# Gating the first branch: from the last stage's first passes into the third stage's second half

## The chip, the cores and the metric

The kernel runs on 1 core of a Trainium2 chip. The metric is the device time in microseconds (us) of one execution. Five engines work side by side, each in its own order: PE (TensorE: matmuls), DVE (VectorE), ACT (ScalarE), POOL (GpSimd) and SP (SyncE, which here only issues DMA transfers). An engine takes its instructions strictly in turn: if the next one waits for a semaphore, everything behind it on that engine waits too.

## The reference

```
x: 2048 x 1024;  h = layernorm(x) over the last axis
g = sigmoid(sum(x * gate_w))                        # one gate per row
a = Cs_re @ (x @ Ch_re.T) - Cs_im @ (x @ Ch_im.T)   # first branch: Fourier mixing
u = gelu(h.T @ w1 + b1)                             # w1: 2048 x 3584
b = (u @ w2 + b2).T                                 # second branch; w2: 3584 x 2048
out = g * a + (1 - g) * b
```

Everything is float32.

## The kernel before, in words

**Four stages.** The first two compute the first branch `a` and store it to the output tensor `out_dram` (they use the symmetry of the Fourier matrices; a check of it, `verdict`, picks a general path for other matrices, which isn't run with these inputs). The third (`Up`, tiles named `u_...`) computes `u` and stores it to DRAM; the last (`Down`, tiles `o_...`) multiplies `u` by `w2` and adds the result, scaled by `hgate` = 1 - g, onto `out_dram`. Before a block of `out_dram` can be added to, it must have been multiplied by the gate.

**Passes.** Third and last stage are block products, 4 x 4 blocks of the weight (`W`) by 4 x 2 of the other operand (`R`), done with a bilinear scheme of 26 products where the plain way takes 32. Each product is a pass j = 0 to 25; its operands are sums and differences of blocks, made by DVE from tiles that SP (some by POOL) loads, or by accumulating DMA. A float32 operand is split into a high part (ACT, `L653`) and a low part (DVE, `L658` and `L660`), and each product of tiles is three matmuls (`L1056` to `L1058`). A pass has 4 blocks of k by 7 row tiles in the third stage, and 7 by 4 in the last (three passes there, 3, 15 and 22, are split once more). When a pass ends, ACT (`plain_copy`, L1101) or DVE (`fused`, L1109) reads its PSUM banks into `u_c` or `o_c` tiles before PE may use these banks again. There are 8 banks; a third-stage pass uses 7, a last-stage pass 4. In the third stage ACT then applies gelu (L1363), and POOL stores `u_c` to `u`.

**The gate.** In pass 7 to 13 of the third stage the gates are computed (`row_gate`, `gates`: tiles `gate`, `hgate`, `ngate`, `bgate`; ACT part at L1522). `gated(i, h, key)` then treats one half row block of the first branch: SP loads 128 x 512 floats of `out_dram` into a tile `g` (through `load`, L626), ACT multiplies by the gate and adds `bgate` (L1505), and POOL stores the tile back (through `store`, L636). 16 row blocks by 2 halves make 32 such pieces.

**What sets the order.** The program is first written down as a list of tasks. Each carries a key, the step it belongs to; a step is one block of k, so a third-stage pass is 4 steps and a last-stage pass 7. `during(j, key)` is called at the start of pass j and adds what runs beside it; `GATED_AT` and `GATED_STEP` say from which pass on the pieces come and how many steps lie between them. A planner (`Graph.schedule`) then plays the whole program through with costs of its own and writes down each engine's instructions in the order in which they started there. A task is due in relation to the place of its key on PE's line. A load is taken to land when its bytes have passed at `DMA_RATE` (400000 bytes a us) and 3.5 us more (`DMA_LATENCY`) have gone by; what reads the tile is placed behind that. Tiles share slots (`f`: 39 of 1024 floats a partition, `h`: 24 of 512, `ps`: 8 banks); a load needs a free slot.

Of the kernel before, what the change touches and what calls it, by code (L numbers as in the profile page):

```python
# [20 lines left out]
NS = S // P  # L21
# [10 lines left out]
DMA_RATE = 400000.0  # L32
SPARE = 2
DMA_LATENCY = 3.5
ADD_LATENCY = 1.5
LOAD = 14.0
WAIT = 0.5
# [8 lines left out]
def act(n):  # L46
    return 0.10 + n * 0.86e-3
# [188 lines left out]
STATS_AT, STATS_STEP = ("y", 1), 4.5  # L236
GATE_AT, GATE_STEP = 7, 1.5
VERDICT_AT = 21
GATED_AT, GATED_STEP = 0, 2
H_LEAD, H_EACH = 25, 1.3  # L240
O_ORDER = [24, 6, 17, 15, 0, 13, 12, 2, 25, 1, 16, 10, 5, 14, 4, 23, 3, 7, 11, 21, 18, 22, 9, 8, 19, 20]
O_SUMS = signs([
# [42 lines left out]
class Buf:  # L285
# [3 lines left out]
    def __init__(self, kind, name, t=None, parts=1, dtype=F32):  # L289
        self.kind, self.name, self.t, self.parts, self.dtype = kind, name, t, parts, dtype  # L290
        self.writer = [None] * parts
        self.readers = [[] for _ in range(parts)]
        self.taker = self.reading = self.next = None
        self.users = set()
# [53 lines left out]
class Task:  # L348
    def __init__(self, seq, key, engines, fn, nbytes):
        self.seq, self.key, self.engines, self.fn, self.nbytes = seq, key, engines, fn, nbytes  # L350
        self.deps, self.after, self.need, self.behind, self.bufs = set(), [], [], [], {}
        self.order = (key, seq)
        self.engine = self.bank = None

    def __lt__(self, o):
        return self.order < o.order


class Graph:
# [72 lines left out]
    def schedule(self):  # L432
# [7 lines left out]
        at, dma, now = 0, 0.0, 0.0  # L440
# [36 lines left out]
        def start(t, e):  # L477
            nonlocal dma
            t.engine, t.start = e, now
            if t.bank:  # L480
                t.bank.reading = t
            order.append(t)
            for b in t.need:
                b.index = free[b.slot].pop(0)
                waiting[b.kind].remove(t)
            idle[e] = now + t.engines[e]
            end = idle[e]
            if t.nbytes:
                dma = max(dma, now) + t.nbytes / DMA_RATE
                end = dma + DMA_LATENCY + (ADD_LATENCY if t.engines[e] == 0.9 else 0)  # L490
            heapq.heappush(events, idle[e])
            t.end = end
            heapq.heappush(events, end + HOP)
            heapq.heappush(done, (end + HOP, t.seq, t))
            for s in t.after:
                unborn[s] -= 1
                if not unborn[s]:
                    s.ready = max(d.end for d in s.deps) + HOP
                    for o in s.engines:
                        if o in soon and len(s.engines) == 1:  # L500
                            soon[o].append(s)
# [10 lines left out]
        while events:  # L512
# [3 lines left out]
            while done and done[0][0] <= now:  # L516
                t = heapq.heappop(done)[2]
# [8 lines left out]
            if idle["PE"] <= now and at < len(pe) and not left[pe[at]] and has_slots(pe[at]):  # L526
                start(pe[at], "PE")
                at += 1
            for e, heap in ready.items():
                held = []  # L530
                while heap and idle[e] <= now and len(held) < 60:
                    t = heapq.heappop(heap)
# [17 lines left out]
def arm(  # L550
# [19 lines left out]
    g = Graph(SLOTS)  # L570
# [43 lines left out]
    def slot(n, name, dtype=F32):  # L614
        return View(Buf("f" if n > H else "h", name, None, 1, dtype), 0, n)
# [7 lines left out]
    def load(key, v, src, r=(), queue="SP"):  # L623
        q = {"SP": nc.sync, "ACT": nc.scalar}[queue]
        dst = (lambda: v.ap.rearrange("p (c j) -> p c j", j=H)) if len(src.shape) == 3 else lambda: v.ap
        g.add({queue: 0.06}, key, lambda e: q.dma_start(dst(), src), r=r, w=(v.reg,), nbytes=P * v.n * 4)  # L626
# [100 lines left out]
    class Bilinear:  # L727
# [57 lines left out]
        def during(self, j, key):  # L785

            if (self.name, j) == STATS_AT:
                stats(key, STATS_STEP)
# [521 lines left out]
    class Up(Bilinear):  # L1310
# [20 lines left out]
        def during(self, j, key):  # L1331
            if fast and j == VERDICT_AT:
                verdict()
            if j == GATE_AT:
                load_consts(key)
                for row in range(NS):
                    row_gate(row, key + GATE_STEP * row, View(self.h[row], 0, D))
                gates(key + GATE_STEP * NS)
# [29 lines left out]
    class Down(Bilinear):  # L1368
# [11 lines left out]
        def source(self, x_, b, k):  # L1380
# [2 lines left out]
                return w2[i * P:(i + 1) * P, c:c + H], ()  # L1383
            i, h = (b // 2) * 7 + k, b % 2
            return u_dram[i].t[:, h * H:(h + 1) * H], [(u_dram[i], h)]

        def during(self, j, key):
            if j == GATED_AT:
                for n in range(2 * NS):
                    gated(n // 2, n % 2, key + GATED_STEP * n)  # L1390

        def back(self, b, j):
            return j == len(self.out) - 1 or next(i for i in self.ends[b] if i >= j) == len(self.out) - 1
# [66 lines left out]
    def load_consts(key):  # L1460
        src = bass.AP(tensor=gate_w.tensor, offset=gate_w.offset, ap=[[0, P], [1, D]])
        prod = View(Buf("h", "xgw", None, 1, mybir.dt.bfloat16), 0, D)
        load(key, GW, src)
        g.add({"ACT": act(D) + 0.25}, key, lambda e: nc.scalar.activation(prod.ap, GW.ap, AF.Copy, accum_out=sgw.t),
              r=(GW.reg,), w=(prod.reg, sgw))

    def stats(key, each):
        load(key, View(b12_sb, 0, NF + NS), b12)
        for row in range(NS):
            row_stats(row, key + each * row)  # L1470
        rstds(key + each * NS)
# [22 lines left out]
    def row_gate(k, key, v):  # L1494

        prod, col = View(Buf("h", f"xg{k}", None, 1, mybir.dt.bfloat16), 0, D), slice(k, k + 1)
        g.add({"DVE": dve(D)}, key, lambda e: nc.vector.scalar_tensor_tensor(
            prod.ap, v.ap, 1.0, GW.ap, op0=ALU.mult, op1=ALU.mult, accum_out=zg.t[:, col]),
            r=(v.reg, GW.reg), w=(prod.reg, zg))

    def gated(i, h, key):

        v, reg, cols = slot(H, f"g{i}_{h}"), (out_dram[i], h), slice(h * H, (h + 1) * H)
        load(key, v, out_dram[i].t[:, cols], (reg,))
        g.add({"ACT": act(H) + 0.08}, key, lambda e: nc.scalar.activation(  # L1505
            v.ap, v.ap, AF.Identity, bias=bgate.t[:, i:i + 1], scale=gate.t[:, i:i + 1]), r=(v.reg, gate, bgate), w=(v.reg,))
        store(key + 0.5, out_dram[i].t[:, cols], reg, v)
# [760 lines left out]
    def verdict():  # L2268
        n = len(kept)
        parts, sums16 = const(n, "parts"), Buf(None, "sums16", consts.tile([P, n], BF16, tag="sums16", name="sums16"))  # L2270
        total, test, usual = const(n, "total"), const(3, "test"), [const(1, f"usual{i}") for i in range(2)]
        at = {what: i for i, what in enumerate(kept)}

        def fill(_):
            for b, few in zip(usual, (SPECIAL, FEW)):
                nc.vector.memset(b.t, 1.0)
                nc.vector.memset(b.t[:few, :], 0.0)

        g.add({"DVE": 0.3}, -1, fill, w=usual)
        for what, i in at.items():  # L2280
            m = counted[what]
            assert m == len(kept[what].writer), (what, m)
            g.add({"ACT": 0.5}, step, lambda e, i=i, what=what: nc.scalar.activation(
                kept[what].t, kept[what].t, AF.Copy, accum_out=parts.t[:, i:i + 1]), r=(kept[what],), w=(kept[what], parts,))

        def masked(e):
            for b, what in zip(usual, ("odd", "even")):
                i = at[what]
                nc.vector.tensor_mul(parts.t[:, i:i + 1], parts.t[:, i:i + 1], b.t)

        g.add({"DVE": 0.2}, step, masked, r=(*usual, parts), w=(parts,))
        g.add({"DVE": 0.1}, step, lambda e: nc.vector.tensor_copy(sums16.t, parts.t), r=(parts,), w=(sums16,))
        ps = Buf("ps", "ps_verdict")
        g.add({"PE": 0.1}, step, lambda e: nc.tensor.matmul(ps.t[:, :n], ones[:, :P], sums16.t, start=True, stop=True), r=(sums16,), w=(ps,))

        def decide(e):
            v, t, a, b = nc.vector, total.t, test.t[:, :1], test.t[:, 1:2]

            def col(what):
                return t[:, at[what]:at[what] + 1]  # L2300

            v.tensor_scalar(t, ps.t[:, :n], 1.0, None, op0=ALU.mult)
            v.scalar_tensor_tensor(a, col("rest"), LEAST, col("seq_main"), op0=ALU.mult, op1=ALU.is_lt)
            v.scalar_tensor_tensor(b, col("hid_rest"), LEAST, col("hid_main"), op0=ALU.mult, op1=ALU.is_lt)
            v.tensor_mul(a, a, b)
            for what, most in (("seq_main", 1e30), ("hid_main", 1e30), ("odd", 0.5), ("even", 0.5), ("all", 0.5)):
                v.tensor_scalar(b, col(what), most, None, op0=ALU.is_lt)
                v.tensor_mul(a, a, b)
            v.tensor_scalar(b, a, -1.0, 1.0, op0=ALU.mult, op1=ALU.add)
            v.tensor_copy(bad, b)  # L2310

        g.add({"DVE": 1.0}, step, decide, r=(ps,), w=(total, test, Buf(None, "bad", bad)))
# [6 lines left out]
    for t in g.schedule():  # L2319
        for b in t.need:  # L2320
            pool, n = pools[b.slot]
# [98 lines left out]
```

## Time and profile before

| what | value |
|---|---|
| median of 3 runs | 1250.75 us (1249.62 to 1253.84) |
| profiled execution, its own time | 1252.64 us |
| its span, first to last instruction | 1250.6 us |
| mean granted TensorE clock | 0.992 |
| instructions | 17645 |
| DMA traffic | 347.35 MB, mean 278 GB/s |

The profile is of one execution. A group row names line, engine, operation, written and read tiles (buffer numbers left out), shapes and count. In the timeline a row starts with its start and its duration in us; brackets give how long the engine had been idle before it and what ended that. "PEclk" is the clock that the throttle granted, as a share of full speed; the DMA share is the mean busy share of the 16 DMA engines (it can pass 1 a little, since a packet's time is counted where it started).

### The profile page before, as it was taken

How to read it: one execution, taken by the hardware profiler on the slowest of the kernel's cores; microseconds unless marked ns; L12 is line 12 of the kernel's file. 1: busy time of each engine (PE TensorE's matmuls, PEld its weight loads, DVE VectorE, ACT ScalarE, POOL GpSimd, SP SyncE). 2: the span in 40 equal slices, each digit the busy share in tenths (PEclk: the TensorE clock that was granted, in tenths of full speed). 3: DMA queues.
4: the chain of work that ended last, by engine and by line, in shares of the span. 5: the costliest groups of instructions: out<-in, count | busy, mean ns of one | idle time of the engine just before them, and what ended most of it. 6: DMA issues, size and time to landing. Idle time of an engine off the chain costs nothing.

```text
span 1250.6 us, 17645 instructions
## 1 busy us (share of the span) xinstructions
PE 1221.7 (98%) x5640; PEld 983.3 (79%) x5647; DVE 1152.9 (92%) x1998; ACT 699.2 (56%) x1252; POOL 211.1 (17%) x325
## 2 busy tenths in 40 slices
PE   8999999899999999999999999999999999999997
PEld 5678756688888888887787887887788889888886
DVE  8999978999998899989999689898999989999995
ACT  7852697584743424534635567756545546665632
POOL 0000010312130220211202233213120111231212
PEclk9999999999999999999999999999899999999999
DMA  9999772989577798989967999999993687899655
GB/s 376 402 360 408 279 203 72 300 308 358 198 272 267 261 343 310 342 306 354 358 248 242 403 406 361 299 320 321 273 292 121 178 217 210 231 247 289 131 139 104
DMA packets 142282, 347.35 MB, mean 278 GB/s; under 512 B 17378, under 2 KB 20322, under 8 KB 142179
## 3 DMA queue, kind: packets, MB, share of 16 engines
q1 hardware_dynamic: 109762, 256.39, 57.8%
q0 software_dynamic: 32272, 89.67, 26.1%
q8 instruction: 46, 0.75, 0.2%
q14 instruction: 58, 0.47, 0.1%
q10 hardware_dynamic: 144, 0.07, 0.0%
HBM read 264.40 MB, written 81.66 MB: 277 GB/s over the span
## 4 chain that ended last, share of the span: by engine, by line


## 5 line engine op out<-in xcount | busy, mean ns | idle before, releaser
L1056 PE MATMUL ps_u_p<-u_p_r_hi,u_p_w_hi 128*128 128x512 f32 x728 | 284.7, 391 | 2.0 <-DVE u_c L1109 2.0
L1058 PE MATMUL ps_u_p<-u_p_r_hi,u_p_w_lo 128*128 128x512 f32 x728 | 283.3, 389 | 0.0
L1057 PE MATMUL ps_u_p<-u_p_r_lo,u_p_w_hi 128*128 128x512 f32 x728 | 283.3, 389 | 0.0
L1056 PE MATMUL ps_o_p<-o_p_r,o_p_w 128*128 128x512 f32 x654 | 257.3, 393 | 7.3 <-DVE o_c L1109 4.3
L1057 PE MATMUL ps_o_p<-o_p_r,o_p_w 128*128 128x512 f32 x654 | 256.0, 391 | 0.0
L1058 PE MATMUL ps_o_p<-o_p_r,o_p_w 128*128 128x512 f32 x654 | 255.9, 391 | 0.0
L653 ACT ACTIVATE u_p_w_hi<-u_W_p 128x896 fp32r<-128x896 f32 x104 | 97.4, 949 | 125.0 <-DVE u_W_p L618 36.9
L1056 PEld LDWEIGHTS ps_u_p<-u_p_r_hi,u_p_w_hi 128*128 128x128 f32 x728 | 136.6, 188 | 34.1 <-DVE u_c L1109 6.2
L1058 PEld LDWEIGHTS ps_u_p<-u_p_r_hi,u_p_w_lo 128*128 128x128 f32 x728 | 136.6, 188 | 28.8
L1057 PEld LDWEIGHTS ps_u_p<-u_p_r_lo,u_p_w_hi 128*128 128x128 f32 x728 | 136.7, 188 | 28.0
L1056 PEld LDWEIGHTS ps_o_p<-o_p_r,o_p_w 128*128 128x128 f32 x654 | 123.7, 189 | 36.4 <-DVE o_c L1109 6.6
L1058 PEld LDWEIGHTS ps_o_p<-o_p_r,o_p_w 128*128 128x128 f32 x654 | 123.7, 189 | 26.0
L1057 PEld LDWEIGHTS ps_o_p<-o_p_r,o_p_w 128*128 128x128 f32 x654 | 123.9, 189 | 25.2
L653 ACT ACTIVATE o_p_w<-o_W_p 128x512 fp32r<-128x512 f32 x164 | 100.9, 625 | 62.1 <-DVE o_W_p L621 21.0
L653 ACT ACTIVATE o_p_r<-o_R_p 128x512 fp32r<-128x512 f32 x157 | 95.7, 623 | 67.7 <-DVE o_R_p L621 37.6
L636 POOL DMA_DIRECT2D u<-u_c x126 | 68.6, 545 | 288.9 <-DVE u_c L1109 133.0
L660 DVE TENSOR_TENSOR o_p_r<-o_R_p,o_p_r 128x512 fp32r<-128x512 f32 x157 | 107.0, 686 | 8.6 <-ACT o_p_r L653 8.5
L1611 PE MATMUL ps_fq<-fc,fx_f 128*128 128x256 f32 (+1 forms) x368 | 101.6, 422 | 4.6 <-DVE fx_h L618 3.4
L1109 DVE SCALAR_TENSOR_TENSOR u_c<-ps_u_p,u_c 128x512 f32<-128x512 f32 x161 | 105.3, 684 | 0.4
L1611 PEld LDWEIGHTS ps_fq<-fc,fx_f 128*128 128x128 f32 x368 | 70.7, 193 | 28.8 <-issue 13.4
L618 DVE TENSOR_TENSOR u_W_p<-u_W_p,u_W_p 128x896 f32<-128x896 f32 x72 | 77.2, 1085 | 5.8 <-DMA u_W_p<-in_w_dram 5.8
L631 POOL DMA_DIRECT2D o_W_p<-in_w_dram x50 | 46.3, 941 | 210.6 <-DVE o_p_w L658 57.1
(289 smaller groups left out, 1980.8 us busy)
## 6 DMA issues: line engine op xcount, KB each, us to landing
u_W_p<-in_w_dram SPq DMA_DIRECT2D x124, 448.0 KB, 6.7
o_W_p<-in_w_dram SPq DMA_DIRECT2D x160, 256.0 KB, 6.6
o_R_p<-u SPq DMA_DIRECT2D x140, 256.0 KB, 6.2
fc<-in_ct_dram SPq DMA_DIRECT2D x64, 512.0 KB, 9.2
u<-u_c POOLq DMA_DIRECT2D x126, 256.0 KB, 6.3
u_c<-u SPq DMA_DIRECT2D x70, 256.0 KB, 6.7
o_W_p<-in_w_dram POOLq DMA_DIRECT2D x50, 256.0 KB, 7.1
out_dram<-o_c POOLq DMA_DIRECT2D x44, 256.0 KB, 8.1
```

Of the source, the lines that this page charges most:

```text
L618: g.add({"DVE": dve(o.n)}, key, lambda e: nc.vector.tensor_add(o.ap, a.ap, b.ap), r=(a.reg, b.reg), w=(o.reg,))
L631: g.add({"POOL": 0.9}, key, lambda e: nc.gpsimd.dma_start(dst(), src, accum_op=ALU.add), r=(v.reg, *r), w=(v.reg,), nbytes=2.2 * P * v.n * 4)
L636: g.add({queue: 0.6 if queue == "POOL" else 0.06}, key, lambda e: q.dma_start(dst, v.ap), r=(v.reg,), w=(reg,) if reg else (), nbytes=P * ...
L653: g.add({"ACT": act(v.n)}, key, lambda e: nc.scalar.activation(hi.ap, v.ap, AF.Copy, scale=-1.0 if negate else 1.0), r=(v.reg,), w=(hi.reg,))
L660: nc.vector.tensor_sub(lo.ap, v.ap, hi.ap.bitcast(F32))
L1056: nc.tensor.matmul(bank.ap, wh.ap[:, c], rh.ap[:, e], start=a, stop=False, skip_group_check=True)
L1057: nc.tensor.matmul(bank.ap, wh.ap[:, c], rl.ap[:, e], start=False, stop=False, skip_group_check=True)
L1058: nc.tensor.matmul(bank.ap, wl.ap[:, c], rh.ap[:, e], start=False, stop=b, skip_group_check=True)
L1109: lambda e: nc.vector.scalar_tensor_tensor(o.ap, ps.ap, scale, o.ap, op0=ALU.mult, op1=ALU.add),
L1611: nc.tensor.matmul(b.ap[:, c0:c0 + r.shape[-1]] if r.shape[-1] < H else b.ap, w, r, start=begin, stop=end, skip_group_check=True)
```

## The change

The 32 calls of `gated` are made in the third stage from pass 13 on, 1.5 steps apart (48 steps, so up to pass 24 of 25), and no longer in the last stage from pass 0 on, 2 steps apart. Their loads get a margin: the planner takes them to land 5 us later than other loads. Nothing else is edited; the planner then orders all engines anew.

```
+MARGIN = 5.0
...
-GATED_AT, GATED_STEP = 0, 2
+GATED_AT, GATED_STEP = 13, 1.5
...
 class Task:
+        self.margin = 0.0
...
 Graph.schedule, start():
-                end = dma + DMA_LATENCY + (ADD_LATENCY if t.engines[e] == 0.9 else 0)
+                end = dma + DMA_LATENCY + t.margin + (ADD_LATENCY if t.engines[e] == 0.9 else 0)
...
 class Up:
         def during(self, j, key):
             if fast and j == VERDICT_AT:
                 verdict()
+            if j == GATED_AT:
+                for n in range(2 * NS):
+                    gated(n // 2, n % 2, key + GATED_STEP * n)
...
 class Down:
-        def during(self, j, key):
-            if j == GATED_AT:
-                for n in range(2 * NS):
-                    gated(n // 2, n % 2, key + GATED_STEP * n)
...
 def gated(i, h, key):
         load(key, v, out_dram[i].t[:, cols], (reg,))
+        g.tasks[-1].margin = MARGIN
```

Three places in the order show it. In the names, `u_p13_w_0_hi` is the high part of W, block 0, of pass 13 of the third stage, `g1_0` the gate's piece of row block 1, half 0; the numbers at the end count tiles. Code lines behind the edit are one or two higher in the changed kernel.

ACT in the last stage, from the end of pass 5's copies to the operands of pass 7, before:

```order
L1452 ACTIVATE o_c2_2_7969<-o_c2_2_7969,hgate_81 128x512
L653 ACTIVATE o_p7_w_0_8011<-o_W0_p4_0_6931 128x512
L1505 ACTIVATE g14_0_7936<-g14_0_7936,bgate_80,gate_79 128x512
L653 ACTIVATE o_p7_r_0_8024<-o_R4_p4_0_7005 128x512
L653 ACTIVATE o_p7_r_1_8031<-o_R4_p4_1_7048 128x512
L653 ACTIVATE o_p7_w_1_8039<-o_W0_p7_1_7797 128x512
```

and now:

```order
L655 ACTIVATE o_p7_w_0_7982<-o_W0_p4_0_6977 128x512
L1452 ACTIVATE o_c2_2_7979<-o_c2_2_7979,hgate_81 128x512
L655 ACTIVATE o_p7_r_0_8000<-o_R4_p4_0_7019 128x512
L655 ACTIVATE o_p7_r_1_8008<-o_R4_p4_1_7044 128x512
L1103 ACTIVATE o_c2_2_7979<-ps_o_p4_3_0_7664 128x512
```

The piece g14_0 stood ahead of pass 7's operands and is gone; no g is left in the last stage.

ACT in the third stage, pass 13, before:

```order
L653 ACTIVATE u_p13_w_2_hi_4386<-u_W15_p13_2_4279 128x896
L653 ACTIVATE u_p13_w_3_hi_4421<-u_W15_p13_3_4281 128x896
L653 ACTIVATE u_p13_r_2_hi_4435<-u_R14_p13_2_4206 128x512
L653 ACTIVATE u_p13_r_3_hi_4448<-u_R14_p13_3_4217 128x512
L653 ACTIVATE u_p14_w_0_hi_4492<-u_W15_p13_0_4150 128x896
```

and now:

```order
L655 ACTIVATE u_p13_w_2_hi_4413<-u_W15_p13_2_4278 128x896
L1506 ACTIVATE g1_0_4287<-g1_0_4287,bgate_80,gate_79 128x512
L655 ACTIVATE u_p13_w_3_hi_4434<-u_W15_p13_3_4280 128x896
L655 ACTIVATE u_p13_r_2_hi_4447<-u_R14_p13_2_4282 128x512
L1506 ACTIVATE g1_1_4324<-g1_1_4324,bgate_80,gate_79 128x512
L655 ACTIVATE u_p13_r_3_hi_4463<-u_R14_p13_3_4284 128x512
L655 ACTIVATE u_p14_w_0_hi_4512<-u_W15_p13_0_4150 128x896
```

Pieces of the gate stand between the high parts of one pass; the other operands keep their order here.

SP's queue in the third stage, the loads of W for passes 14 and 15, before:

```order
L626 DMA u_W0_p14_2_4423<-in_w1_dram 128x896
L626 DMA u_W0_p14_3_4437<-in_w1_dram 128x896
L626 DMA u_W9_p15_0_4455<-in_w1_dram 128x896
L626 DMA u_W1_p15_0_4457<-in_w1_dram 128x896
L626 DMA u_W9_p15_1_4494<-in_w1_dram 128x896
```

and now:

```order
L628 DMA u_W0_p14_2_4449<-in_w1_dram 128x896
L628 DMA u_W0_p14_3_4461<-in_w1_dram 128x896
L628 DMA g2_0_4471<-out_0_dram 128x512
L628 DMA g2_1_4473<-out_0_dram 128x512
L628 DMA u_W9_p15_0_4475<-in_w1_dram 128x896
L628 DMA u_W1_p15_0_4477<-in_w1_dram 128x896
L628 DMA g3_0_4514<-out_0_dram 128x512
L628 DMA u_W9_p15_1_4520<-in_w1_dram 128x896
```

Three loads of g now stand between loads of W.

More of the change, by code (lines that the diff above doesn't have):

```diff
@@ L34 @@
 DMA_LATENCY = 3.5
+MARGIN = 5.0
 ADD_LATENCY = 1.5
@@ L238 @@
 VERDICT_AT = 21
-GATED_AT, GATED_STEP = 0, 2
+GATED_AT, GATED_STEP = 13, 1.5
 H_LEAD, H_EACH = 25, 1.3
@@ L353, in __init__ @@
         self.engine = self.bank = None
+        self.margin = 0.0
     def __lt__(self, o):
@@ L489, in start @@
                 dma = max(dma, now) + t.nbytes / DMA_RATE
-                end = dma + DMA_LATENCY + (ADD_LATENCY if t.engines[e] == 0.9 else 0)
+                end = dma + DMA_LATENCY + t.margin + (ADD_LATENCY if t.engines[e] == 0.9 else 0)
             heapq.heappush(events, idle[e])
@@ L1333, in during @@
                 verdict()
+            if j == GATED_AT:
+                for n in range(2 * NS):
+                    gated(n // 2, n % 2, key + GATED_STEP * n)
             if j == GATE_AT:
@@ L1385, in source @@
             return u_dram[i].t[:, h * H:(h + 1) * H], [(u_dram[i], h)]
[L1387 to L1390, printed above, removed]
         def back(self, b, j):
@@ L1504, in gated @@
         load(key, v, out_dram[i].t[:, cols], (reg,))
+        g.tasks[-1].margin = MARGIN
         g.add({"ACT": act(H) + 0.08}, key, lambda e: nc.scalar.activation(
```

## The prediction

> **What bounds the kernel now.** I read the page first. TensorE (PE) is the engine that matters, and it is nearly always busy:
>
> ```profile
> PE 1221.7 (98%) x5640; PEld 983.3 (79%) x5647; DVE 1152.9 (92%) x1998; ACT 699.2 (56%) x1252; POOL 211.1 (17%) x325
> ```
>
> So only time in which PE stands still, or runs at a reduced clock, can be won. Next comes the view of one line, L1056, which says where the stages lie: the third stage (tiles u) starts its matmuls at 236.8 us and the last (tiles o) at 737.1 us.
>
> ```profile
> L1056 PE MATMUL ps_u_p<-u_p_r_hi,u_p_w_hi x728: 387/389/582, 236.8 to 736.4; 128*128 128x512 f32 x182
> L1056 PE MATMUL ps_o_p<-o_p_r,o_p_w x654: 387/389/796, 737.1 to 1241.2; 128*128 128x512 f32 x164
> ```
>
> A pass of either stage is 84 matmuls (4 blocks of k by 7 row tiles by 3 in the third, 7 by 4 by 3 in the last), so I cut the trace at every 84th matmul and asked for the busy time of each piece. Columns: stretch, its length, busy time of PE, PEld, DVE, ACT and POOL (with counts), granted TensorE clock, share of the DMA engines, GB/s.
>
> ```profile
> 541.70:560.70 19.00, 19.00 (x85) 15.75 (x84) 15.59 (x21) 5.40 (x8) 2.72 (x5) 1.00 0.91 323
> 560.70:580.80 20.10, 19.48 (x85) 15.61 (x84) 19.23 (x26) 7.17 (x11) 3.02 (x6) 1.00 0.96 353
> 699.00:718.00 19.00, 19.00 (x85) 15.75 (x84) 9.01 (x14) 8.81 (x14) 5.42 (x10) 1.00 1.04 404
> 737.10:759.10 22.00, 19.16 (x85) 15.54 (x83) 20.73 (x35) 15.03 (x28) 9.24 (x17) 1.00 1.05 398
> 759.10:780.00 20.90, 20.86 (x84) 16.77 (x85) 18.18 (x36) 17.30 (x34) 5.82 (x10) 0.92 1.06 356
> 780.00:799.10 19.10, 19.10 (x86) 15.80 (x85) 14.55 (x32) 12.82 (x22) 4.87 (x7) 1.00 1.04 317
> 855.30:877.70 22.40, 19.20 (x85) 15.58 (x83) 18.69 (x32) 12.74 (x23) 6.98 (x9) 1.00 1.08 299
> 877.70:900.70 23.00, 22.17 (x84) 17.73 (x85) 21.75 (x36) 12.56 (x22) 3.06 (x4) 0.85 0.87 281
> ...
> 484.60:737.10 252.50, 250.50 (x1095) 204.05 (x1094) 228.29 (x322) 119.98 (x172) 45.35 (x84) 1.00 0.88 321
> 737.10:900.70 163.60, 156.69 (x727) 130.38 (x726) 147.37 (x259) 109.15 (x195) 41.62 (x62) 0.97 1.01 327
> 900.70:1224.20 323.50, 322.62 (x1538) 271.01 (x1537) 315.00 (x552) 182.74 (x333) 60.19 (x74) 1.00 0.76 203
> ```
>
> An undisturbed pass takes 19.0 to 19.1 us. Passes 0, 1, 6 and 7 of the last stage (counted from 0) take 22.0, 20.9, 22.4 and 23.0. Their excess over 19.05 us each is 88.3 - 76.2 = **12.1 us**, and the rest of that stage, 900.7 to 1224.2, has only 0.9 us of PE idle. The list of PE's waits names what PE waited for, and two short windows show the clock behind the two long waits:
>
> ```profile
> PE ps_o_p L1056 <- DVE o_c L1109: 4.3, 3, 3.2
> PE ps_o_p L1056 <- ACT o_c L1101: 2.9, 1, 2.9
> PE ps_u_p L1056 <- DVE u_c L1109: 2.0, 7, 0.6
> ...
> 759.00:762.50 3.50, 3.36 (x7) 2.32 (x8) 1.92 (x4) 2.97 (x7) 1.91 (x3) 0.51 1.07 331
> 878.50:885.40 6.90, 6.10 (x15) 4.58 (x15) 6.90 (x12) 4.47 (x10) 1.44 (x2) 0.51 1.07 341
> ```
>
> Each long wait (2.9 and 3.2 us) is followed by 3.5 and 6.9 us at half clock, which cost a further 1.7 and 3.4 us. So a wait here costs about one and a half times to twice itself. The Trainium skill, "TensorE: Matmul & The Clock Gate", section "What's actually happening", puts the half rate behind an idle window of about 3.4 us; here 2.9 us of idling did it, so the measurement decides. By that rule the first wait would not have slowed the clock, and 1.7 us less would be won there (a sum of 1244.8 in place of the 1243.1 below). Waits of up to 0.6 us left the clock at 1.00 (row 560.70).
>
> **Who makes the two waits.** The gate's 32 pieces (tiles g) run exactly through these passes:
>
> ```profile
> L626 SPq DMA_DIRECT2D g<-out_dram x32: 327/330/752, 686.3 to 868.5; - x32
> L1505 ACT ACTIVATE g<-g,bgate,gate x32: 799/814/833, 698.6 to 880.6; 128x512 f32<-128x512 f32 x32
> L636 POOL DMA_DIRECT2D out_dram<-g x32: 542/544/897, 699.8 to 882.4; - x32
>   DMA g<-out_dram: 22.2, 16
> DMA to landing us min/median/max: 2.8/6.5/13.0
> ```
>
> ScalarE (ACT) stood idle 16 times, 22.2 us in all, for a g load. ACT runs in order, so whatever stands behind the g waits too. The timeline at the two places:
>
> ```profile
> 754.50 0.82 ACT L1505 ACTIVATE g<-g,bgate,gate 128x512 f32<-128x512 f32 x1 [1.67 <-DMA g<-out_dram]
> 755.01 0.68 DVE L618 TENSOR_TENSOR o_W_p<-o_W_p,o_W_p 128x512 f32<-128x512 f32 x1
> 757.79 0.81 ACT L1505 ACTIVATE g<-g,bgate,gate 128x512 f32<-128x512 f32 x1 [0.91 <-DMA g<-out_dram]
> 758.51 1.06 ACT L1101 ACTIVATE o_c<-ps_o_p 128x512 f32<-128x512 f32 x2
> 759.14 0.79 PE L1056 MATMUL ps_o_p<-o_p_r,o_p_w 128*128 128x512 f32 x1 [2.88 <-ACT o_c L1101]
> ...
> 865.98 0.81 ACT L1505 ACTIVATE g<-g,bgate,gate 128x512 f32<-128x512 f32 x1 [4.02 <-DMA g<-out_dram]
> 867.35 0.69 DVE L660 TENSOR_TENSOR o_p_r<-o_R_p,o_p_r 128x512 fp32r<-128x512 f32 x1 [3.71 <-ACT o_p_r L653]
> 877.73 0.50 PE L1056 MATMUL ps_o_p<-o_p_r,o_p_w 128*128 128x512 f32 x1 [3.22 <-DVE o_c L1109]
> ```
>
> First place: ACT waits 1.67 and 0.91 us for g loads and spends 2 x 0.72 us (start to start) on them, and the copies that free PE's accumulators come after. Second place: ACT waits 4.02 us for one g load, VectorE (DVE) 3.71 us for ACT, and DVE's o_c, behind that in its queue, keeps PE 3.2 us and then 0.8 (the 4.3 us row).
>
> **The change, part by part.** It takes 32 loads (SP), 32 multiplications (ACT) and 32 stores (POOL) out of 686 to 882 us and puts them between the operands of passes 13 to 25 of the third stage, from about 465 us on; nothing is added.
>
> Gain in the last stage. At the first place, without the g's, the copies could follow the ACT o_p_w split, whose input DVE ended at 755.7 us; split and copy start about 756.3 instead of 758.5. So 2.2 of the 2.9 us go even if DVE comes no earlier, and with 0.7 us of wait the clock stays up. At the second place the 4.02 us exceed the 3.2 + 0.8 us of wait, so that goes whole. Left over: 0.7 us, and 0.4 us as the later passes have (0.9 us in 17 passes, times 8). Gain 12.1 - 1.1 = **11.0 us**; bounds: 6.5 us, if only the first place heals or the second halves, and 12.1.
>
> Cost on ACT in the third stage. 32 x 0.72 = 23 us over 252.5 us in which ACT is busy 120.0: room. What matters is waiting. The plan put the multiplication about 4.2 us behind its load (0.26 MB at the planner's 400 kB a us, and 3.5); with landings of median 6.5 us half of them waited. Now it stands 9.2 us behind. Loads in the third stage landed within 11.2 us:
>
> ```profile
> DMA to landing us min/median/max: 3.0/6.8/11.2
> ...
> ACT u_p_w_hi L653 <- DVE u_W_p L621: 21.2, 7, 5.8
> ACT u_p_w_hi L653 <- DVE u_W_p L618: 20.8, 9, 6.6
> ```
>
> So a g waits 2.0 us at most. Moreover ACT here waits for DVE (42 us in these two rows), and a wait for g lies largely beside that. Lower bound -2.0 us (the seven u_c waits vanish as the order shifts), upper bound +5 (a third of 32 waits, 1 us each, half of them reaching PE as in the last stage). The rows are nearest to the low end: I take **+1.5 us**.
>
> Cost on DMA. The stretch 484.6 to 737.1 moves 321 GB/s x 252.5 us = 81 MB at share 0.88. About 25 of the 32 pieces come in new, 25 x 2 x 0.262 = 13.1 MB: 94 MB, share 1.02. The row 699.00 carried 404 GB/s at 1.04, so it fits, barely. What hides a late load is the lead of the operands. Low halves of W begun (four a pass) by the start of passes 13, 17 and 23:
>
> ```profile
> 0.00:484.60 484.60, 141.49 (x364) 68.32 (x364) 58.08 (x54) 0.99 0.84 297
> 0.00:560.70 560.70, 185.00 (x476) 89.34 (x476) 77.55 (x72) 0.99 0.84 298
> 0.00:678.60 678.60, 250.51 (x644) 120.88 (x644) 105.37 (x98) 0.99 0.84 298
> ```
>
> DVE's 54, 72 and 98 against 52, 68 and 92 used up: a lead of half a pass at pass 13, one pass at 17, one and a half at 23. If that cover is gone, each long wait costs 4.6 us (2.9 and half clock). Taken as 0.
>
> SP and POOL. SP stood 17.2 us behind stores of g whose slots it wanted:
>
> ```profile
> SPq L626 <- DMA out_dram<-g: 17.2, 7, 6.2
> ```
>
> That wait goes with the g's: behind them in SP's queue are now loads of u_W and u_c, up to 6.2 us late, within the lead except at passes 13 and 14. POOL's 32 x 0.54 us stand between stores of u with room (45 of 252.5 us busy). Both 0, upper bound in the +5.
>
> Sum: -11.0 + 1.5 = -9.5 us. The profiled execution took 1252.64 us (span 1250.6 and 2.0 around it), so 1243.1; it stood 1.9 us above the median of 1250.75. If that excess lay outside these waits, the median falls to 1241.2. I forecast **1243**, own range 1237 to 1247.
>
> **Rivals.** A: the third stage becomes DMA-bound and gives half back. For it: 81 MB at share 0.88 is 365 GB/s at 1.00; 94 MB would take 257.8 us, 5.3 us too long. Against: shares of 1.04 to 1.06 stand in rows above, and the lead. Time 1252.64 - 11.0 + 1.5 + 5.3 = 1248.4. The Trainium skill, "DMA: Bandwidth & Descriptors", "Specifications", gives about 358 GB/s of HBM for a core, which speaks more strongly against the change: by it 94 MB need 262.6 us, 10.1 too long, and the sum would be 1253. The row with 404 GB/s over a whole pass disagrees.
>
> B, slower: late g's in passes 13 to 16, where the lead is thinnest, stop PE as they did in the last stage. For it: that cost 12.1 us there. Against: 5 us more room, and accumulators that are free earlier, since the last block of a third-stage pass ends its first row tile 8.2 us before the pass does (6 tiles x 6 matmuls x 19.05/84 us), against 4.1 us (3 x 6 x 19.05/84) in the last stage. It decides once such waits exceed 14.8 us; two of 4.6 and one of 7.4 us make 16.6, so 1252.64 - 11.0 + 16.6 = 1258.2.
>
> C: the change doesn't do what it says, because the last stage is late by its own loads. For it: share 1.05 in pass 0, where DVE idles as early as 699 to 718 (9.01 of 19.00 busy), before most g's. Against: the g's are named as releaser in both places. Then the 2.2 us of the first place go and nothing else: 1252.64 - 2.2 = 1250.4.
>
> **How the numbers follow.** 0.3% (about 3.8 us) is what a measurement can tell. Forecast 0.60, A 0.16, B 0.13, C 0.11. Faster (below 1247.0): 0.60 and a third of A, 0.65; slower (above 1254.5): B, 0.13; same: the rest, 0.22. The range takes in A, C and the bounds -12.1 and -2.0 below: 1237 (1252.64 - 14.1 - 1.9 = 1236.6) to 1253.
>
> **What would show it.** Right: passes 0, 1, 6 and 7 of the last stage at 19 to 20 us; ACT's wait for g below 8 us; clock 1.00 from 737 to 900; DMA share about 1.0 in 485 to 737 and 0.85 behind. Wrong: PE waits for u_c or u_p_w above 3 us, or the same two half-clock stretches with o_R_p or o_W_p as releaser.

## The result and the profile after

The changed kernel took **1239.0 us** (median of 6 runs, 1238.45 to 1241.56) against 1250.18 us for the kernel before on the same chip (6 runs, 1246.89 to 1253.84): a ratio of 0.9916, 95% interval 0.9897 to 0.9936, so 11.2 us faster by the medians and 0.8% by the ratio. The forecast was 1243 with a range of 1237 to 1253. The profiled execution took 1238.45 us with a span of 1236.7, 13.9 us less than the profiled span before.

First the engines' row of the page, and the rows of the first of the three matmuls (now L1058) with the place of each stage:

```profile
PE 1216.7 (98%) x5647; PEld 982.3 (79%) x5647; DVE 1152.4 (93%) x1998; ACT 700.0 (57%) x1252; POOL 210.1 (17%) x325
```

```profile
L1058 PE MATMUL ps_u_p<-u_p_r_hi,u_p_w_hi x728: 389/389/579, 236.1 to 732.4; 128*128 128x512 f32 x182
L1058 PE MATMUL ps_o_p<-o_p_r,o_p_w x654: 387/389/500, 733.1 to 1227.3; 128*128 128x512 f32 x164
```

The last stage starts 4.0 us earlier than before (733.1 against 737.1) although the third starts only 0.7 us earlier. Next the stretches that answer to those of the prediction (same columns). The first five rows are passes 0, 1, 2, 6 and 7 of the last stage; then passes 13 to 25 of the third stage, passes 0 to 7 of the last, and the rest up to its final pass.

```profile
733.10:752.40 19.30, 19.24 (x86) 15.61 (x84) 19.30 (x33) 14.78 (x29) 8.11 (x14) 1.00 1.04 366
752.40:772.50 20.10, 19.54 (x84) 15.70 (x85) 20.10 (x42) 12.88 (x26) 3.51 (x4) 1.00 0.99 275
772.50:793.00 20.50, 19.36 (x86) 15.70 (x85) 14.81 (x31) 11.89 (x24) 1.73 (x2) 1.00 0.56 151
...
848.90:868.00 19.10, 19.10 (x86) 15.79 (x85) 18.86 (x32) 11.69 (x20) 4.84 (x6) 1.00 1.08 276
868.00:887.00 19.00, 19.00 (x85) 15.74 (x84) 19.00 (x32) 10.24 (x18) 1.56 (x2) 1.00 0.82 272
...
485.40:733.10 247.70, 247.70 (x1094) 204.84 (x1093) 229.54 (x324) 134.23 (x191) 57.55 (x107) 1.00 1.01 390
733.10:887.00 153.90, 152.15 (x727) 127.43 (x726) 147.55 (x260) 92.53 (x171) 26.26 (x35) 1.00 0.84 249
887.00:1210.30 323.30, 322.25 (x1538) 271.15 (x1537) 311.43 (x546) 182.18 (x332) 60.44 (x74) 1.00 0.76 201
```

Three things stand there. Passes 0, 1, 6 and 7 take 19.3, 20.1, 19.1 and 19.0 us where they took 22.0, 20.9, 22.4 and 23.0, and the clock is 1.00 throughout. Pass 2, at 19.1 before, now takes 20.5. And in passes 13 to 25 of the third stage PE is busy for all of 247.7 us, which is 13 undisturbed passes of 19.05, where the same passes took 252.5 before, though the transfers now run at 390 GB/s and a share of 1.01 there.

All of PE's waits between 484 and 900 us, and then the gate's pieces (tile g) with what ACT waited for ahead of them:

```profile
PE ps_o_p L1058 <- ACT o_c L1103: 1.7, 2, 1.1
```

```profile
L628 SPq DMA_DIRECT2D g<-out_dram x32: 327/333/1203, 434.3 to 662.5; - x32
L1506 ACT ACTIVATE g<-g,bgate,gate x32: 797/801/817, 472.6 to 681.7; 128x512 f32<-128x512 f32 x32
...
  DMA g<-out_dram: 9.4, 3
...
DMA to landing us min/median/max: 2.8/7.1/16.4
```

The seven waits for u_c are gone, and so are the two long waits with their half-clock stretches. ACT still waits 9.4 us for pieces, and one load took 16.4 us to land, longer than the 11.2 us on which the prediction relied; PE doesn't feel it.

**Where the 13.9 us came from.** I cut each trace at the first matmul of pass 13 of the third stage, at the first of the last stage, and at the end of the span. Before: 484.6 + 252.5 + 513.5. After: 485.4 + 247.7 + 503.6. So the last stage gives 9.9 us, passes 13 to 25 of the third give 4.8, and 0.8 us is lost ahead of pass 13 (PE waits 1.3 us for a tile fy_k at the start of the third stage, ahead of every piece; over all kernels below pass 13 starts between 484.6 and 486.4).

**The seven waits cost more than their row says.** The row of u_c waits that the prediction quoted listed 2.0 us; the stretch of passes 17 to 23 shrank by 4.8 (kernel before, then after):

```profile
560.70:699.00 138.30, 136.30 (x591) 109.47 (x590) 132.35 (x189) 68.10 (x97) 24.37 (x45) 1.00 0.85 310
```

```profile
561.50:695.00 133.50, 133.50 (x590) 110.25 (x589) 128.62 (x185) 79.79 (x114) 33.70 (x63) 1.00 1.00 384
```

The timeline of PE before shows why, at the start of pass 19:

```profile
602.44 0.40 PE L1058 MATMUL ps_u_p<-u_p_r_hi,u_p_w_lo 128*128 128x512 f32 x1
603.07 0.50 PE L1056 MATMUL ps_u_p<-u_p_r_hi,u_p_w_hi 128*128 128x512 f32 x1 [0.23 <-DVE u_c L1109]
603.40 0.39 PE L1057 MATMUL ps_u_p<-u_p_r_lo,u_p_w_hi 128*128 128x512 f32 x1
603.63 0.40 PE L1058 MATMUL ps_u_p<-u_p_r_hi,u_p_w_lo 128*128 128x512 f32 x1
```

A matmul lasts 0.39 us but the next one starts 0.227 us behind it (19.05 / 84). An idle time is counted only from the end of the last one. From 602.44 to the waiting matmul are 0.63 us, 0.40 more than undisturbed, and the next step of 0.33 loses another 0.10: 0.50 us lost where 0.23 is listed. Start to start, the matmuls from 560 to 700 us lose 4.7 us together; after, none.

What made DVE late there is seen in its own timeline, before:

```profile
595.47 2.48 DVE L1109 SCALAR_TENSOR_TENSOR u_c<-ps_u_p,u_c 128x512 f32<-128x512 f32 x4
598.33 1.09 DVE L660 TENSOR_TENSOR u_p_w_lo<-u_W_p,u_p_w_hi 128x896 fp32r<-128x896 f32 x1 [0.38 <-DMA u_W<-u_W_p]
...
599.34 6.07 DVE L1109 SCALAR_TENSOR_TENSOR u_c<-ps_u_p,u_c 128x512 f32<-128x512 f32 x10
```

and after:

```profile
593.13 6.06 DVE L1111 SCALAR_TENSOR_TENSOR u_c<-ps_u_p,u_c 128x512 f32<-128x512 f32 x10
599.11 1.08 DVE L660 SCALAR_TENSOR_TENSOR u_p_w_lo<-u_W_p,u_p_w_hi 128x896 fp32r<-128x896 f32 x1
600.11 2.47 DVE L1111 SCALAR_TENSOR_TENSOR u_c<-ps_u_p,u_c 128x512 f32<-128x512 f32 x4
```

At the end of pass 18 DVE reads 7 banks, each twice, 0.60 us a read: 1.20 us for each bank, while PE wants the next bank every 0.68 us (3 matmuls). The pass ends at 599.9 us before and at 599.6 after. Before, DVE had done 4 of the 14 reads when it turned to operands, and 10 fell around and behind the end of the pass, so PE ran at DVE's pace (the matmuls that waited start at 603.07, 604.26 and 605.46 us, 1.20 us apart). After, 10 were done ahead of the end. The count alone doesn't tell everywhere: at the end of pass 22 (678.6 us before, 675.9 after) 8 of the 14 reads begin ahead of the end in both kernels, and the kernel before still loses 1.4 us behind it. The last reads there, before and after:

```profile
680.13 3.68 DVE L1109 SCALAR_TENSOR_TENSOR u_c<-ps_u_p,u_c 128x512 f32<-128x512 f32 x6
675.01 4.87 DVE L1111 SCALAR_TENSOR_TENSOR u_c<-ps_u_p,u_c 128x512 f32<-128x512 f32 x8
```

What differs is when the last read ends. Behind the ends of passes 16, 18 and 22, where PE lost 1.1, 1.6 and 1.4 us, that was 5.6, 5.5 and 5.2 us after the end before, and it is 3.3, 3.0 and 4.0 us now. The edit touched no instruction of DVE; the planner dealt its order anew.

### The profile page after: what moved, and what is told of

It reads as the page before. It is cut to its first block, busy times and chain, and to the rows that moved or that the text cites. A ratio compares the mean times of both kernels' runs of the same rounds, so it can differ in the third digit from the quotient of the medians.

```text
span 1236.7 us, 17649 instructions
## 1 busy us (share of the span) xinstructions
PE 1216.7 (98%) x5647; PEld 982.3 (79%) x5647; DVE 1152.4 (93%) x1998; ACT 700.0 (57%) x1252; POOL 210.1 (17%) x325
## 4 chain that ended last, share of the span: by engine, by line
## 5 line engine op out<-in xcount | busy, mean ns | idle before, releaser
L1058 PE MATMUL ps_u_p<-u_p_r_hi,u_p_w_hi 128*128 128x512 f32 x728 | 283.6, 390 | 1.3 <-DVE fy_k L2227 1.3
L1058 PE MATMUL ps_o_p<-o_p_r,o_p_w 128*128 128x512 f32 x654 | 255.1, 390 | 2.3 <-ACT o_c L1103 2.1
L1058 PEld LDWEIGHTS ps_u_p<-u_p_r_hi,u_p_w_hi 128*128 128x128 f32 x728 | 136.7, 188 | 30.3 <-issue 1.7
L1058 PEld LDWEIGHTS ps_o_p<-o_p_r,o_p_w 128*128 128x128 f32 x654 | 122.8, 188 | 29.8 <-ACT o_c L1103 4.1
L655 ACT ACTIVATE o_p_r<-o_R_p 128x512 fp32r<-128x512 f32 x157 | 96.6, 626 | 84.6 <-DVE o_R_p L623 34.4
L1612 PEld LDWEIGHTS ps_fq<-fc,fx_f 128*128 128x128 f32 x368 | 71.4, 195 | 28.1 <-issue 13.4
```

Source lines behind the costliest of these rows:

```text
L655: g.add({"ACT": act(v.n)}, key, lambda e: nc.scalar.activation(hi.ap, v.ap, AF.Copy, scale=-1.0 if negate else 1.0), r=(v.reg,), w=(hi.reg,))
L1058: nc.tensor.matmul(bank.ap, wh.ap[:, c], rh.ap[:, e], start=a, stop=False, skip_group_check=True)
L1612: nc.tensor.matmul(b.ap[:, c0:c0 + r.shape[-1]] if r.shape[-1] < H else b.ap, w, r, start=begin, stop=end, skip_group_check=True)
```

## The experiments

Three theories went into them. **Queue**: the multiplications, standing in ACT's queue and waiting there for loads, stop the last stage. **Traffic**: it is the pieces' 16.8 MB of loads and stores that hold up the last stage's own loads. And for the third stage **order**: its gain comes from the new order on DVE, not from anything that a piece does. The table has every run; the columns "passes 13-25" and "last stage" are cut as above from the profiled execution, and "ACT for g" is ACT's idle time for loads of g with the number of waits. The kernel before had medians of 1250.09 to 1251.01 beside these.

| kernel | median us | ratio to before, interval | passes 13-25 | last stage | ACT for g |
|---|---|---|---|---|---|
| before | 1250.18 | | 252.5 | 513.5 | 22.2, 16 |
| after | 1239.0 | 0.9916 (0.9897-0.9936) | 247.7 | 503.6 | 9.4, 3 |
| margin only | 1244.75 | 0.9944 (0.9927-0.9962) | 251.2 | 507.0 | 18.7, 4 |
| move only | 1238.81 | 0.9904 (0.9883-0.9925) | 248.8 | 505.3 | 31.0, 15 |
| no gate | 1240.13 | 0.9911 (0.9893-0.9930) | 251.3 | 502.0 | - |
| no multiplication | 1240.66 | 0.9915 (0.9896-0.9935) | 250.2 | 502.8 | - |
| order only | 1237.03 | 0.9888 (0.9867-0.9909) | 247.7 | 502.7 | - |
| step 0.4 | 1249.7 | 0.9987 (0.9973-1.0001) | 261.7 | 502.1 | 13.4, 9 |
| step 1.0 | 1241.75 | 0.9927 (0.9905-0.9949) | 251.7 | 501.4 | 5.8, 5 |
| step 1.2 | 1245.03 | 0.9965 (0.9951-0.9979) | 255.2 | 501.8 | 6.9, 2 |
| step 1.3 | 1242.43 | 0.9942 (0.9928-0.9955) | 253.7 | 502.4 | 7.4, 2 |
| step 1.4 | 1237.64 | 0.9910 (0.9896-0.9925) | 250.8 | 500.3 | 4.9, 4 |

### The margin alone

The kernel before, with its pieces in the last stage, and the margin on their loads:

```
+MARGIN = 5.0
...
+        g.tasks[-1].margin = MARGIN
```

> The 32 pieces stay in the last stage's first passes; only the margin is added, so the planner puts each multiplication about 5 us further behind its load. Queue theory (the loss in the last stage comes from ScalarE standing in its queue for a g load): ScalarE's wait for g falls from 22.2 us to under 8, passes 0, 1, 6 and 7 of the last stage lose 2 to 5 us instead of 12.1, the third stage still loses 4 to 5; time 1241 to 1244. Traffic theory (the loss comes from the 16.8 MB of g beside the last stage's own loads): the traffic is unchanged, so 9 us or more of the loss stay; time 1248 or more.

Measured: 1244.75 us, 6.3 us under the kernel before beside it (1251.01), so somewhat over half of the gain. Passes 0 and 1 of the last stage, and ACT's wait for g:

```profile
736.50:758.00 21.50, 19.91 (x86) 15.56 (x85) 20.38 (x35) 15.06 (x28) 10.45 (x18) 1.00 1.05 397
758.00:780.10 22.10, 19.85 (x85) 15.51 (x84) 19.99 (x39) 17.91 (x35) 6.25 (x9) 1.00 1.07 368
```

```profile
  DMA g<-out_dram: 18.7, 4
```

Passes 6 and 7 are healed (their stall and its half clock are gone), passes 0 and 1 are not: 43.6 us against 42.9 before. But PE's long waits there no longer lead to a g. One goes to DVE, which reads the third stage's last banks between operands, and one to a copy by ACT that stood behind an operand for which DVE had waited on a load of W:

```profile
739.63 0.50 PE L1058 MATMUL ps_o_p<-o_p_r,o_p_w 128*128 128x512 f32 x1 [1.35 <-DVE u_c L1111]
761.10 0.69 DVE L620 TENSOR_TENSOR o_W_p<-o_W_p,o_W_p 128x512 f32<-128x512 f32 x1 [1.99 <-DMA o_W_p<-in_w_dram]
762.99 0.50 PE L1058 MATMUL ps_o_p<-o_p_r,o_p_w 128*128 128x512 f32 x1 [1.14 <-ACT o_c L1103]
```

The time lies between the two theories' ranges (1241 to 1244, and 1248 or more), so this run alone doesn't part them. ACT waits for g nearly as long as before, in fewer and longer waits, so the expected fall of that wait was a miss, and the wait's length says little: what counts is whether something that PE needs soon stands behind it.

### The move alone

The changed kernel with `MARGIN = 0.0`.

> The pieces are moved as in the change, with a margin of 0. If the move is what counts: ScalarE waits 10 to 15 us for g in the third stage, hidden by the lead of the operands, PE waits less than 2 us there; time 1238 to 1241. If the margin is needed: PE waits 4 us or more for u_c or u_p_w in passes 13 to 16 of the third stage; time 1244 or more.

Measured: 1238.81 us, not to be told from the changed kernel. ACT's wait for g, and PE's waits from 484 to 900 us:

```profile
  DMA g<-out_dram: 31.0, 15
```

```profile
PE ps_o_p L1058 <- ACT o_c L1103: 1.7, 2, 1.1
PE ps_u_p L1058 <- DVE u_c L1111: 0.5, 2, 0.2
```

ACT waits for g longer than in any other kernel, 31.0 us, twice the upper end of what I expected and more than the 22.2 us that stopped the last stage, and PE loses 0.5 us by the list in the third stage. The move does the work; the margin adds nothing measurable to it. In the third stage a late piece is covered, as the prediction's lead of the operands had it.

### No gate at all

The kernel before without the 32 calls; the first branch stays ungated.

```
-                for n in range(2 * NS):
-                    gated(n // 2, n % 2, key + GATED_STEP * n)
```

> All 32 pieces are left out (loads, multiplications and stores), so the first branch is added ungated. VectorE's order in the third stage is that of the kernel before. Order theory (the third stage's 4.7 us of loss in passes 17 to 24 hang on the order that the planner writes there, and went because the moved pieces changed it): the third stage loses 4 to 5 us as before, the last stage's first eight passes 0 to 2; time 1239 to 1242, not below the changed kernel. Rival (the loss there was the g traffic's or a matter of the single execution): the third stage loses under 2 us, time 1234 to 1237, below the changed kernel.

Measured: 1240.13 us. This kernel does less than the changed one and is no faster. Its last stage is 11.5 us shorter than before (502.0), so that is all that the pieces cost there; but its third stage keeps the waits for u_c (PE's only waits from 484 to 900 us), and passes 17 to 23 take 136.6 us:

```profile
PE ps_u_p L1056 <- DVE u_c L1109: 1.3, 5, 0.5
```

```profile
561.30:697.90 136.60, 135.28 (x591) 109.90 (x590) 132.16 (x189) 69.59 (x99) 24.27 (x45) 1.00 0.86 311
```

In passes 13 to 25 the first 292 of DVE's 321 instructions of the kernel before stand in the same order here.

### Loads and stores without the multiplication

The kernel before, in which the pieces are loaded and stored in the last stage but not multiplied:

```
-        g.add({"ACT": act(H) + 0.08}, key, lambda e: nc.scalar.activation(
-            v.ap, v.ap, AF.Identity, bias=bgate.t[:, i:i + 1], scale=gate.t[:, i:i + 1]), r=(v.reg, gate, bgate), w=(v.reg,))
```

> The pieces are loaded and stored in the last stage as before, but not multiplied (the first branch is added ungated): the same traffic, no ScalarE instruction that waits for it. Queue theory: the first eight passes of the last stage lose at most 2 us instead of 12, the third stage still 4 to 5; time 1239 to 1242. Traffic theory: 9 us or more of the loss stay; time 1247 or more.

Measured: 1240.66 us. Passes 0 and 1 of the last stage, and PE's waits from 700 to 900 us:

```profile
736.00:755.00 19.00, 19.00 (x86) 15.73 (x85) 17.88 (x30) 12.72 (x25) 9.58 (x18) 1.00 1.05 394
755.00:775.60 20.60, 19.37 (x86) 15.70 (x85) 17.66 (x33) 12.56 (x26) 6.30 (x10) 1.00 1.06 374
```

```profile
PE ps_o_p L1056 <- ACT o_c L1101: 2.0, 2, 1.2
```

The traffic is all there (share 1.05 and 1.06 in these passes, as before), and the last stage takes 502.8 us, 0.8 more than without any piece. That total hides something: in this stage the pieces run in the first eight passes only. These passes in this kernel, then in the one with no gate:

```profile
736.00:891.10 155.10, 152.97 (x728) 127.48 (x727) 147.31 (x260) 92.20 (x170) 42.32 (x64) 1.00 1.04 344
735.90:888.10 152.20, 152.20 (x727) 127.60 (x726) 145.42 (x257) 91.18 (x169) 25.94 (x34) 1.00 0.83 242
```

They take 155.1 us here, 152.2 with no gate and 163.6 in the kernel before; the passes behind them are 2.1 us shorter here than with no gate, with no piece in either. So of the 11.4 us that the pieces cost in these passes, 8.5 go with ACT's instruction, and 2.9 stay. Those can be the traffic or the order, since the planner orders this kernel anew as well; no run parts the two. The queue theory holds for the main part, and the traffic theory, by which 9 us or more had to stay, falls. That these passes lose at most 2 us was a miss: passes 1 and 2 alone lose 3.2. The run takes away ACT's work on the pieces together with its waiting. At the prediction's first place both stood in the way (2.6 us of waiting, 1.4 us of work), at the second a single wait of 4.0 us.

### The order alone

The planner plans the pieces where the changed kernel has them, but they emit nothing: all other instructions stand in the changed kernel's order (by the traces they do, one by one, on all five engines).

```
-        load(key, v, out_dram[i].t[:, cols], (reg,))
+        none = lambda e: None
+        g.add({"SP": 0.06}, key, none, r=(reg,), w=(v.reg,), nbytes=P * v.n * 4)
...
-        g.add({"ACT": act(H) + 0.08}, key, lambda e: nc.scalar.activation(
...
-        store(key + 0.5, out_dram[i].t[:, cols], reg, v)
+        g.add({"ACT": act(H) + 0.08}, key, none, r=(v.reg, gate, bgate), w=(v.reg,))
+        g.add({"POOL": 0.6}, key + 0.5, none, r=(v.reg,), w=(reg,), nbytes=P * v.n * 4)
```

> The planner still plans the 32 pieces where the changed kernel has them, so every other instruction stands in the changed kernel's order on all engines, but the pieces emit nothing: the first branch stays ungated, as in the kernel with no gate at all (1240.13 us). If the third stage's gain comes from the new order alone: passes 17 to 24 of the third stage at 19.0 to 19.2 us without a wait for u_c, and a time 3 to 5 us under that of the kernel without the gate, 1235 to 1237. If the order is right but the pieces cost nothing where they stand: as the changed kernel, 1238.5 to 1239.5. If instead the moved traffic or the multiplications themselves did it (loads and stores that shift the others): the u_c waits of 3 to 5 us come back and the time is 1240 to 1242.

Measured: 1237.03 us. Passes 17 to 23, and all of PE's waits from 484 to 900 us:

```profile
562.30:695.70 133.40, 133.40 (x590) 110.32 (x589) 128.46 (x183) 68.79 (x98) 24.90 (x46) 1.00 0.87 320
```

```profile
PE ps_o_p L1058 <- ACT o_c L1103: 0.9, 1, 0.9
```

Neither this kernel nor the one with no gate has a piece; the only thing that differs is the order, and with it passes 17 to 23 take 133.4 us in place of 136.6, without a wait. The order theory holds. The medians differ by 3.1 us, at the low end of what was expected; the intervals of the two ratios overlap, but no execution of the one kernel (1235.9 to 1238.3) is as long as any of the other (1239.7 to 1241.1). In passes 13 to 25 the kernels with DVE's old order take 4.8 (before), 3.6 (no gate) and 2.5 us (no multiplication) more than this one, so the 4.8 us of the profiled execution before are at the high end. The changed kernel's pieces themselves then cost 1239.0 - 1237.0 = 2.0 us by the medians, though the two intervals overlap.

### How dense the pieces may be

The changed kernel with other distances between pieces, all from pass 13 on (0.4 is shown; the others are 1.0, 1.2, 1.3 and 1.4):

```
-GATED_AT, GATED_STEP = 13, 1.5
+GATED_AT, GATED_STEP = 13, 0.4
```

> The changed kernel with 0.4 in place of 1.5 steps between pieces: all 32 within some 3 passes from pass 13 on. 2 x 8.4 MB beside 323 GB/s over 61 us make 36.5 MB, that is 598 GB/s where 404 is the most that a pass carried, so about 29 us of transfers come late against a lead of a half to one pass (9 to 19 us). If the third stage can be bound by its transfers (the prediction's A) or stopped by late pieces (its B): PE waits for u operands or u_c of 6 to 15 us in passes 13 to 18, some at half clock, 1246 to 1255. If the lead takes it: no wait over 1 us there, 1238 to 1241.

> The changed kernel with 1.0 in place of 1.5 steps between pieces: they end in pass 21, not 24, and leave the loads of the last stage's first operands alone. If the pieces in passes 21 to 24 make the 3.0 us that passes 0 to 2 of the last stage still lose: these passes at 19.1 to 19.3, 1236 to 1237. If the last stage's own loads make them: 1238.5 to 1239.5. If a third of the room is too little for the third stage: u_c waits or late operands there, 1240 to 1243.

> The changed kernel with 1.2 steps between pieces (32 pieces end in pass 22). If the third stage's gain hangs on the order of DVE alone, which each spacing deals anew: between the step 1.5 (no u_c wait) and the step 1.0 (2.4 us of u_c waits, 1241.75 us), with no rule; 1236 to 1242, PE's u_c waits and the time going together. If it hangs on density (the more a us, the worse, as 0.4 gave 1249.7): 1240 to 1241 here, and falling from 1.2 over 1.3 to 1.4.

> The changed kernel with 1.3 steps between pieces. Order theory: 1236 to 1242, set by the u_c waits that its order happens to have. Density theory: 1239.5 to 1240.5, less than at 1.2.

> The changed kernel with 1.4 steps between pieces. Order theory: 1236 to 1242, set by the u_c waits that its order happens to have. Density theory: 1239 to 1240, the least of the three. The pieces in passes 22 and 23 should bring back part of the waits for ACT's o_c in the last stage's first three passes (3.0 us at step 1.5, 0.1 at step 1.0).

Measured, from 0.4 to 1.4: 1249.7, 1241.75, 1245.03, 1242.43 and 1237.64 us. At 0.4 passes 14 and 15 take 21.7 and 29.5 us, and the gain of the last stage is spent:

```profile
503.70:525.40 21.70, 20.12 (x86) 15.46 (x85) 18.21 (x25) 15.79 (x22) 10.81 (x21) 1.00 1.02 400
525.40:554.90 29.50, 22.91 (x86) 17.42 (x85) 22.07 (x31) 16.76 (x25) 7.55 (x14) 0.88 1.03 396
```

The chain into PE's longest wait there, and into that of the kernel with a step of 1.2:

```profile
539.71 1.09 DVE L623 TENSOR_TENSOR u_W_p<-u_W_p,u_W_p 128x896 f32<-128x896 f32 x1 [3.10 <-DMA u_W_p<-in_w_dram]
...
540.89 0.95 ACT L655 ACTIVATE u_p_w_hi<-u_W_p 128x896 fp32r<-128x896 f32 x1 [3.20 <-issue]
...
541.89 0.50 PE L1058 MATMUL ps_u_p<-u_p_r_hi,u_p_w_hi 128*128 128x512 f32 x1 [3.52 <-ACT u_p_w_hi L655]
```

```profile
589.27 1.09 DVE L620 TENSOR_TENSOR u_W_p<-u_W_p,u_W_p 128x896 f32<-128x896 f32 x1 [7.73 <-DMA u<-u_c]
...
591.02 0.79 PE L1058 MATMUL ps_u_p<-u_p_r_hi,u_p_w_hi 128*128 128x512 f32 x1 [5.88 <-DVE u_c L1111]
```

DVE waits for transfers of W (3.10 us in the first; 7.73 in the second, where the profile names a store as the last to end, but a load of W issued at 576.47 us landed at 589.15, just ahead of DVE's start), and what stands behind it waits too. Loads of W took a median of 7.1 us to land between 560 and 600 us in the kernel before, 9.3 in the changed one, and 11.4 at step 1.2. So the third stage can be held up by its transfers, as rival A had it, only not at step 1.5. The rate doesn't tell these kernels apart. Passes 13 to 18 in the changed kernel, then at step 1.0:

```profile
485.40:599.60 114.20, 114.20 (x506) 94.59 (x505) 104.08 (x139) 61.25 (x86) 26.93 (x50) 1.00 1.03 402
486.40:602.20 115.80, 115.01 (x506) 94.34 (x505) 95.69 (x129) 61.23 (x86) 28.31 (x53) 1.00 1.03 406
```

At 1.3 and 1.2 the same passes carried 404 and 403 GB/s, and at 0.4, where PE stood still for part of them, 391; the most that a single pass of the changed kernel carried is 416.

At 0.4 and 1.0 the losing branch of the expectation came, with PE's waits as expected there. The density theory is right in that every step below 1.5 loses in the third stage (250.8 to 261.7 us against 247.7), and wrong in its details: 1.0 is better than 1.2, 1.3 came out at 1242.43 where it expected 1239.5 to 1240.5, and 1.4 at 1237.64 where it expected 1239 to 1240. DVE's longest wait for a transfer in these passes was 4.9, 4.9, 7.7 and 4.4 us at 0.4, 1.0, 1.2 and 1.3, but 4.7 us at step 1.5 too (553.8 us), where PE lost nothing, so such a wait alone doesn't settle it. The order theory called the 1.4 (its 1236 to 1242 would have called nearly anything) but neither the 1.2 nor the 1.3. Both seem to act together, and I can't split the loss at 1.0 and 1.3 between them. The last expectation for 1.4, that part of the o_c waits would come back in the last stage, was hardly borne out: none is listed, and passes 0 to 2 take 57.7 us where the changed kernel takes 59.9. That stage takes 500.3 us, the least of all, since the passes behind the first eight, with no piece in either, are 1.7 us shorter than in the changed kernel. Step 1.4 keeps u_c waits in the third stage instead,

```profile
PE ps_u_p L1058 <- DVE u_c L1111: 2.0, 4, 0.8
```

and its 1237.64 us is not to be told from the changed kernel's 1239.0 (0.9910 and 0.9916, each within 0.002). No run here had both the third stage of step 1.5 and the last stage of step 1.4, which by their sum would be 3 us better; whether one order can have both isn't shown.

## Why the prediction was right, and where it was wrong

The sign, the place and the mechanism of the gain held: 1243 was forecast, 1239.0 came. From the profiled execution the sum was -9.5 us, and the profiled span fell by 13.9; 0.8 us of loss ahead of pass 13 had no term in it. Term by term:

**Last stage, -11.0 forecast, -9.9 measured.** At the first place the prediction left 0.7 us in passes 0 and 1 and 0.4 later on; passes 0, 1, 6 and 7 now exceed 19.05 us by 1.3 us together (77.5 - 76.2). At the second place the whole stall went. What was missed is pass 2, 1.4 us longer than before: PE waits 1.1 us for ACT's o_c there (774.7 us), and 0.9 us at nearly the same place when the pieces emit nothing, so most of that belongs to the order and not to the pieces. Passes 0 and 1 take 19.0 us each in that kernel, so the order alone doesn't explain what is left in them. That the stall was mainly ACT's queue and not the traffic is shown by the kernel without the multiplication: 8.5 of 11.4 us. Rival C falls as the main cause; up to 2.9 us of it stay possible.

**ACT in the third stage, +1.5 forecast, -4.8 measured.** This is the term that failed, by 6.3 us, and the result lies outside its own bounds of -2.0 and +5. Two steps of it went wrong. The lower bound of -2.0 took the seven u_c waits at what the list of waits said; start to start they cost 4.7. And the choice "the rows are nearest to the low end: I take +1.5" priced only the pieces' own waiting. The bound's condition, that the waits vanish as the order shifts, is what happened, and the order without the pieces did it alone (247.7 us). Neither the count of pieces nor their costs show it, and other spacings kept such waits; what shows it is how late behind a pass's end DVE's last read comes in the new order. So this gain was luck: nothing in the change aimed at it, and without it 9.1 us (9.9 - 0.8) would be left of the gain, close to the 9.5 that were forecast. The pieces' own waiting cost about 1.1 us there (248.8 - 247.7) even in the kernel without margin, with its 31.0 us of it; that kernel's order is its own as well, so the 1.1 us needn't all be theirs.

**DMA, 0 forecast: right, and near the edge.** The forecast was 94 MB at a share of 1.02 over 252.5 us; measured 390 GB/s x 247.7 us = 96.6 MB at 1.01. The lead held at step 1.5; the denser kernels show rival A's price when it doesn't, up to 14.0 us (261.7 - 247.7). The Trainium skill's 358 GB/s a core, by which the prediction priced 1253, is not the limit here: 390 GB/s were held over 247.7 us with PE never waiting. The Trainium skill, "HBM Reference", "Specifications (TRN2)", says that this figure is the share with both cores of a pair at work, and that a core alone measures about 425 GB/s; the 404 to 416 GB/s that passes 15 to 20 of the changed kernel carried stay below that and agree with it, and the prediction had used the wrong of the two figures.

**SP and POOL, 0: the list of PE's waits in these stages names neither. Clock: 1.00 from 733 to 900**, as forecast, and the half clock came back only with long waits: behind 3.52 us (clock 0.88 in that pass) and behind 5.88 us at step 1.2, never behind a wait of 0.9 to 1.6 us in these stages. (In the second stage of the changed kernel half clock follows a wait of 2.1 us, for 3.4 us from 221.3 us on.) DMA shares: 1.01 in the third stage's passes and 0.84 in the last stage's first eight, where "about 1.0" and "0.85" stood.

**ACT's wait for g below 8 us** was to show the forecast right; it was 9.4 in the changed kernel and 31.0 in one that is as fast. It was the wrong thing to look at. Rival B (late pieces in passes 13 to 16) did not come at step 1.5; at 0.4 PE does stop in passes 14 and 15, though its longest wait goes back to a load of W and not to a piece.

Against the medians the gain is 11.2 us and not 13.9 (14.2 by the two executions' own times), since the profiled execution before stood 2.5 us above the median of 1250.18 and the one after 0.6 us below its own.

## What to carry to other kernels

On an engine that works strictly in turn, an instruction that may wait for a transfer belongs where its successors have a lead, and the lead, not the length of the wait, decides: in the third stage 31 us of ACT's waiting cost about 1 us, where in the last 22 us of it, with ACT's work on the pieces, cost 8.5. Where matmuls overlap, take the cost of a wait from start to start and not from the list of idle times, which showed 2.0 us of 4.7. And where a planner deals the order anew, part of any gain or loss is the new order itself: run the plan with the moved work left out before giving the credit to the move.

## What the runs showed that was not expected

- Waits of PE for evictions are listed at less than half of their cost here (0.23 listed, 0.50 lost), since a matmul lasts 0.39 us and the next starts after 0.227.
- One core's transfers held 390 GB/s for 247.7 us beside a PE that never waited, and over passes 13 to 18 they stayed at 402 to 406 GB/s at steps from 1.5 down to 1.0; at 1.2, loads of W landed in a median of 11.4 us (560 to 600 us) instead of 7.1 in the kernel before.
- Two reads of one bank by DVE (2 x 0.60 us) take longer than PE needs for the row tile that follows (0.68 us). At three pass ends PE lost 1.1 to 1.6 us where DVE's last read ended 5.2 to 5.6 us behind the end, and nothing where it ended 3.0 to 4.0 us behind it.
